# A scale-and-add kernel: HBM split in blocks of 72 and 56 rows, with a new order of loads and stores

## The chip, the cores and the metric

The kernel runs on one core of one Trainium2 chip. The metric is the device time of one execution in microseconds. Three runs of the kernel before gave 119.58, 119.69 and 119.91 us, a median of 119.69 us.

## What is computed

```python
B, S, D = 1024, 16, 512
x = normal(B, S, D) * 0.05          # bf16
y = normal(B, S, D) * 0.05          # bf16
gamma = 1e-4 * (normal(D) * 0.05)   # bf16

def reference(x, y, gamma):
    return x + gamma * y
```

With its first two dimensions flattened, each of `x`, `y` and the output is a matrix of 16,384 rows of 512 bf16 values, 1 KB a row and 16.78 MB a matrix. Two matrices are read and one is written: 50.33 MB.

## The kernel before

The 16,384 rows are shared out over the 128 partitions, 128 rows each. In this text "rows 4 to 68" means rows 4 to 68 of every partition, so a transfer of 64 rows moves 64 KB for each partition, 8.39 MB in all.

**Blocks.** `BLOCKS` (line 7) says which rows of HBM belong to a partition. The matrix is cut into three blocks of 4, 64 and 60 rows a partition. Within a block a partition's rows lie next to each other, so a transfer inside one block is one contiguous run for each partition. The function `rows_of` makes this view and asserts that a transfer stays within a block. As the work is elementwise, any such split gives the same output as long as `x`, `y` and the output use the same one.

**Transfers.** Two engines issue DMAs, each in the order of a list written out by hand. `SP` (lines 12 to 19) is the SyncE's: all of `y` and nearly all of `x`. `ACT` (line 20) is ScalarE's: the first four rows of `x`, `gamma`, and the three stores. An `x` entry has a fourth number, the row of the buffer `x_sb` at which it is placed. `x_sb` has 76 rows only, so the later loads of `x` overwrite rows that an addition has read. `y_sb` holds all 128 rows and is also where the result is made. `ring` (line 113) issues the lists and puts the waits in front: a load of `x` waits until the additions that free its place are done (`frees`), and a store waits until the additions of its own rows are done, both by counting the semaphore `s_add` in the order of the additions. `EARLY` moves the first two of SP's DMAs and the first of ScalarE's to the very start of the program, ahead of the start barrier.

**Hold and release.** `HOLD` names the load `y` 0 to 4. TensorE waits for its landing (line 147) and then raises one semaphore each for SP, ScalarE and VectorE (lines 148 and 149). SP's third DMA and ScalarE's second (`AHEAD`) wait for it. `RELEASE` names the load `x` 68 to 120. TensorE waits for its landing (line 157) and then raises `s_go`, for which the first store waits, and `s_rel`, for which VectorE waits.

**Compute.** `gamma` is copied to all partitions once: a matmul with a row of ones (line 152) and a copy out of PSUM (line 154). All other arithmetic is VectorE's. `PIECES` (line 9) cuts the 128 rows into pieces of 8, 16, 44, 52 and 8 rows, and the list `DVE` gives the order: `('m', c)` multiplies piece `c` of `y` by gamma in place (line 180), `('a', c)` adds `x` to it (line 189). The order is m0, m1, m2, a2, a0, a1, m3, m4, a3, a4.

Of the kernel before, what the change touches and what calls it, by code (L numbers as in the profile page):

```python
# [3 lines left out]

BLOCKS = [4, 64, 60]

PIECES = [8, 16, 44, 52, 8]


SP = [
    ('y', 0, 4),
    ('y', 4, 68),
    ('x', 4, 68, 4),
    ('y', 68, 128),
    ('x', 68, 120, 24),
    ('x', 120, 128, 0),
]
ACT = [('x', 0, 4, 0), ('g',), ('s', 4, 68), ('s', 0, 4), ('s', 68, 128)]  # L20

EARLY = (2, 1)

HOLD, AHEAD = ('y', 0, 4), (2, 1)

RELEASE = ('x', 68, 120, 24)

DVE = [('m', 0), ('m', 1), ('m', 2), ('a', 2), ('a', 0), ('a', 1), ('m', 3), ('m', 4), ('a', 3), ('a', 4)]
MULT, ADD = mybir.AluOpType.mult, mybir.AluOpType.add


def _take(sem, n, eng):


    return eng.wait_ge(sem, n).then_inc(sem, -n)  # L35


def kernel(
# [9 lines left out]
    nc = tc.nc  # L48
# [8 lines left out]
    rows = N // P  # L57
    n = len(PIECES)
    assert sum(PIECES) == rows
    starts = [sum(PIECES[:c]) for c in range(n + 1)]  # L60
    dt = xf.dtype
    edges = [sum(BLOCKS[:c]) for c in range(len(BLOCKS) + 1)]
    assert edges[-1] == rows

    def rows_of(t, a, b):

        c = max(c for c in range(len(BLOCKS)) if edges[c] <= a)
        assert b <= edges[c + 1]
# [6 lines left out]
    y_sb = nc.alloc_sbuf_tensor("y_sb", [P, rows, D], dt).ap()  # L75
    x_loads = [w for w in ACT + SP if w[0] == "x"]
    y_loads = [w for w in SP + ACT if w[0] == "y"]
    stores = [w for w in SP + ACT if w[0] == "s"]
    for loads in (x_loads, y_loads, stores):
# [7 lines left out]
    s_load = {w: sem("s_" + "_".join(map(str, w[:2]))) for w in x_loads + y_loads}  # L87
    s_held = {nc.sync: sem("s_held_sp"), nc.scalar: sem("s_held_act"), nc.vector: sem("s_held_dve")}
    s_add, s_go, s_rel, s_end, s_out = sem("s_add"), sem("s_go"), sem("s_rel"), sem("s_end"), sem("s_out")
    added = [a for kind, *a in DVE if kind == "a"]  # L90
    order = {a[0]: k for k, a in enumerate(added)}

    def meets(a, b, c, d):
        return a < d and c < b
# [4 lines left out]
    def x_at(row):  # L99
        return next(w[3] + row - w[1] for w in x_loads if w[1] <= row < w[2])  # L100
# [12 lines left out]
    def ring(eng, what, n_early, n_ahead):  # L113

        known, went = 0, False
        for k, w in enumerate(what):
            kind = w[0]
            if k == n_ahead:
                _take(s_held[eng], 1, eng)
            need = frees(w) if kind == "x" else pieces_of(w[1], w[2]) + list(w[3:]) if kind == "s" else []  # L120
            need = max((order[c] + 1 for c in need), default=0)
            if kind == "s" and not went:
                _take(s_go, 1, eng)
                went = True
            if need > known:
                eng.wait_ge(s_add, need)
                known = need
            if kind == "g":
                i = eng.dma_start(out=gamma_row, in_=gamma.unsqueeze(0)).then_inc(s_gamma, 16)
            elif kind == "x":  # L130
                to = x_sb[:, w[3] : w[3] + w[2] - w[1], :]
                i = eng.dma_start(out=to, in_=rows_of(xf, w[1], w[2])).then_inc(s_load[w], 16)
            elif kind == "y":
                r = slice(w[1], w[2])
                i = eng.dma_start(out=y_sb[:, r, :], in_=rows_of(yf, w[1], w[2])).then_inc(s_load[w], 16)
            else:
                r = slice(w[1], w[2])
                i = eng.dma_start(out=rows_of(of, w[1], w[2]), in_=y_sb[:, r, :]).then_inc(s_out, 16)
            if k < n_early:
                early.append(i.ins)  # L140

    ring(nc.sync, SP, EARLY[0], AHEAD[0])
    ring(nc.scalar, ACT, EARLY[1], AHEAD[1])


    nc.vector.memset(ones_row, 1.0).then_inc(s_ones, 1)  # L146
    _take(s_load[HOLD], 16, nc.tensor)
    for s_one in s_held.values():
        nc.tensor.sem_inc(s_one, 1)
    _take(s_ones, 1, nc.tensor)  # L150
    _take(s_gamma, 16, nc.tensor)
    nc.tensor.matmul(gamma_ps, ones_row, gamma_row, start=True, stop=True).then_inc(s_ps, 1)  # L152
# [3 lines left out]

    _take(s_load[RELEASE], 16, nc.tensor)
    nc.tensor.sem_inc(s_go, 1)
# [4 lines left out]
    def need(loads, c):  # L163
        for w in loads:
            if w not in landed and meets(starts[c], starts[c + 1], w[1], w[2]):
                if w == RELEASE:
                    _take(s_rel, 1, nc.vector)
                elif w == HOLD:
                    _take(s_held[nc.vector], 1, nc.vector)
                else:  # L170
                    _take(s_load[w], 16, nc.vector)
                landed.add(w)

    for kind, *args in DVE:
        c = args[0]
        yt = y_sb[:, starts[c] : starts[c + 1], :]
        if kind == "m":
            need(y_loads, c)
            g = gamma_sb[:, None, :].to_broadcast([P, PIECES[c], D])
            nc.vector.tensor_tensor(out=yt, in0=yt, in1=g, op=MULT).then_inc(s_dve, 1)  # L180
            open_mults += 1
        else:
# [4 lines left out]
            at = x_at(starts[c])  # L187
            xt = x_sb[:, at : at + PIECES[c], :]
            nc.vector.tensor_tensor(out=yt, in0=xt, in1=yt, op=ADD).then_inc(s_add, 1)  # L189
# [44 lines left out]
```

## Time and profile before

| what | us |
|---|---|
| median of three runs | 119.69 |
| span of the profiled execution, first to last instruction | 118.2 |
| VectorE busy in the span | 70.1 |
| of that, the five multiplies and the five additions | 34.7 each |
| TensorE busy | 0.6 |
| mean DMA rate over the span | 426 GB/s |

The profiled execution's own time is known by its span; what lies around the span, by comparison with the median of the runs, is about 1.5 us. "Busy" counts the arithmetic of an engine, not the issuing of DMAs or the waits. The page's DMA row gives, for 40 equal slices of the span, the mean busy share of the core's 16 DMA engines in tenths.

The timeline gives the issue times, which are needed to read the landings: SP issues `y` 0-4 and `y` 4-68 from 0.00 on, `x` 4-68 at 3.71 and `y` 68-128 at 4.09, and the last two loads of `x` from 55.37 on. ScalarE issues `x` 0-4 at 0.13, `gamma` at 3.90, and the three stores from 77.41 to 94.43. The page's list of DMA issues names each transfer with its size and the time from its issue to its landing; transfers of 64 rows are the ones without a size.

### The profile page before, as it was taken

How to read it: one execution, taken by the hardware profiler on the slowest of the kernel's cores; microseconds unless marked ns; L12 is line 12 of the kernel's file. 1: busy time of each engine (PE TensorE's matmuls, PEld its weight loads, DVE VectorE, ACT ScalarE, POOL GpSimd, SP SyncE). 2: the span in 40 equal slices, each digit the busy share in tenths (PEclk: the TensorE clock that was granted, in tenths of full speed). 3: DMA queues.
4: the chain of work that ended last, by engine and by line, in shares of the span. 5: the costliest groups of instructions: out<-in, count | busy, mean ns of one | idle time of the engine just before them, and what ended most of it. 6: DMA issues, size and time to landing. Idle time of an engine off the chain costs nothing. (4 is left out here: it accounts for less than half of the span.)

```text
span 118.2 us, 91 instructions
## 1 busy us (share of the span) xinstructions
PE 0.6 (0%) x1; PEld 0.1 (0%) x1; DVE 70.1 (59%) x12; POOL 0.2 (0%) x4
## 2 busy tenths in 40 slices
PE   0000100000000000000000000000000000000000
PEld 0000000000000000000000000000000000000000
DVE  0000200089999969999999999999999900000000
POOL 0000000000000000000000000000000000000000
DMA  6999889988899879879969696898899889799793
GB/s 248 461 666 399 355 355 399 665 355 355 355 599 466 355 333 624 374 333 499 499 288 576 288 576 288 360 637 355 355 576 488 355 355 510 333 582 416 333 499 166
DMA packets 1442, 50.33 MB, mean 426 GB/s; under 512 B 161, under 2 KB 162, under 8 KB 546
## 3 DMA queue, kind: packets, MB, share of 16 engines
q1 hardware_dynamic: 864, 33.03, 64.8%
q10 hardware_dynamic: 578, 17.30, 33.9%
HBM read 33.56 MB, written 16.78 MB: 426 GB/s over the span
## 5 line engine op out<-in xcount | busy, mean ns | idle before, releaser
L180 DVE TENSOR_TENSOR y_sb<-y_sb,gamma_sb 128x4096 bf16<-128x4096 bf16 (+3 forms) x5 | 34.7, 6981 | 10.9 <-DVEq L35 10.9
L189 DVE TENSOR_TENSOR y_sb<-x_sb,y_sb 128x4096 bf16<-128x4096 bf16 (+3 forms) x5 | 34.7, 6981 | 1.2 <-DVEq L35 1.1
L154 DVE CAST gamma_sb<-gamma_ps 128x512 bf16<-128x512 f32 x1 | 0.7, 692 | 10.2 <-DVEq L35 10.2
L146 DVE MEMSET ones_row<- 1x128 bf16 x1 | 0.2, 165 | 2.0 <-PEq L51 2.0
L152 PE MATMUL gamma_ps<-gamma_row,ones_row 1*128 1x512 bf16 x1 | 0.6, 581 | 11.6 <-PEq L35 11.6
L152 PEld LDWEIGHTS gamma_ps<-gamma_row,ones_row 1*128 1x128 bf16 x1 | 0.1, 101 | 11.6 <-issue 11.6
L218 POOL MEMSET const-bfloat16-1.0<- 128x1 bf16 x1 | 0.1, 101 | 0.0
L218 POOL MEMSET const-uint8-127<- 128x1 uint8 x1 | 0.1, 101 | 0.0
L218 POOL MEMSET const-float32-0.0<- 128x1 f32 x1 | 0.1, 98 | 0.2 <-issue 0.2
L218 POOL MEMSET const-float32-1.0<- 128x1 f32 x1 | 0.1, 98 | 0.0
## 6 DMA issues: line engine op xcount, KB each, us to landing
y_sb<-in_y_dram SPq DMA_DIRECT2D x1, 7680.0 KB, 57.3
out_dram<-y_sb ACTq DMA_DIRECT2D x1, 7680.0 KB, 23.8
x_sb<-in_x_dram SPq DMA_DIRECT2D x1, 6656.0 KB, 21.7
x_sb<-in_x_dram SPq DMA_DIRECT2D x1, 1024.0 KB, 22.0
y_sb<-in_y_dram SPq DMA_DIRECT2D x1, 512.0 KB, 3.4
x_sb<-in_x_dram ACTq DMA_DIRECT2D x1, 512.0 KB, 4.2
out_dram<-y_sb ACTq DMA_DIRECT2D x1, 512.0 KB, 22.3
y_sb<-in_y_dram SPq DMA_DIRECT2D x1, 23.4
```

The source lines that it names most:

```text
L146: nc.vector.memset(ones_row, 1.0).then_inc(s_ones, 1)
L152: nc.tensor.matmul(gamma_ps, ones_row, gamma_row, start=True, stop=True).then_inc(s_ps, 1)
L154: nc.vector.tensor_copy(out=gamma_sb, in_=gamma_ps).then_inc(s_dve, 1)
L180: nc.vector.tensor_tensor(out=yt, in0=yt, in1=g, op=MULT).then_inc(s_dve, 1)
L189: nc.vector.tensor_tensor(out=yt, in0=xt, in1=yt, op=ADD).then_inc(s_add, 1)
L218: nc = _bacc.Bacc("TRN2", target_bir_lowering=False, num_devices=1)
```

## The change

The blocks become 72 and 56 rows. SP's list begins with `y` 8 to 72 and `x` 8 to 72, which are also its two early DMAs. Then come `y` 72 to 128, `y` 0 to 8, `x` 72 to 128 and `x` 0 to 8. ScalarE's list begins with `gamma`, which is now its early DMA, and has the three stores behind it: 8 to 72, 0 to 8, 72 to 128. There is no `HOLD` any more, so its wait on TensorE, the three raised semaphores and the three waits for them are gone. `RELEASE` names `x` 72 to 128. The pieces are 8, 12, 52 and 56 rows, in the order m1, m2, a2, a1, m3, m0, a3, a0.

```diff
-BLOCKS = [4, 64, 60]
-
-PIECES = [8, 16, 44, 52, 8]
-
+BLOCKS = [72, 56]
+
+PIECES = [8, 12, 52, 56]
 
 SP = [
-    ('y', 0, 4),
-    ('y', 4, 68),
-    ('x', 4, 68, 4),
-    ('y', 68, 128),
-    ('x', 68, 120, 24),
-    ('x', 120, 128, 0),
+    ('y', 8, 72),
+    ('x', 8, 72, 8),
+    ('y', 72, 128),
+    ('y', 0, 8),
+    ('x', 72, 128, 20),
+    ('x', 0, 8, 0),
 ]
-ACT = [('x', 0, 4, 0), ('g',), ('s', 4, 68), ('s', 0, 4), ('s', 68, 128)]
+
+ACT = [('g',), ('s', 8, 72), ('s', 0, 8), ('s', 72, 128)]
 
 EARLY = (2, 1)
 
-HOLD, AHEAD = ('y', 0, 4), (2, 1)
-
-RELEASE = ('x', 68, 120, 24)
-
-DVE = [('m', 0), ('m', 1), ('m', 2), ('a', 2), ('a', 0), ('a', 1), ('m', 3), ('m', 4), ('a', 3), ('a', 4)]
+HOLD = None
+
+AHEAD = (None, None)
+
+RELEASE = ('x', 72, 128, 20)
+
+DVE = [('m', 1), ('m', 2), ('a', 2), ('a', 1), ('m', 3), ('m', 0), ('a', 3), ('a', 0)]
...
-    _take(s_load[HOLD], 16, nc.tensor)
-    for s_one in s_held.values():
-        nc.tensor.sem_inc(s_one, 1)
+    if HOLD:
+        _take(s_load[HOLD], 16, nc.tensor)
+        for s_one in s_held.values():
+            nc.tensor.sem_inc(s_one, 1)
```

From the new lists follow the waits: `x` 72 to 128 waits for the first addition (a2), `x` 0 to 8 for none of its own; the store of 8 to 72 waits for `s_go` and the first two additions, the store of 0 to 8 for all four.

## The prediction

> **What bounds the kernel now.** I read the page from the top down to its DMA rows, then the table of landings, then narrow windows at the opening and at the seams between transfers, and last the VectorE (DVE) groups by form.
>
> ```profile
> span 118.2 us, 91 instructions
> PE 0.6 (0%) x1; PEld 0.1 (0%) x1; DVE 70.1 (59%) x12; POOL 0.2 (0%) x4
> ...
> DMA packets 1442, 50.33 MB, mean 426 GB/s; under 512 B 161, under 2 KB 162, under 8 KB 546
> ```
>
> DVE works 59% of the span; the DMA engines move 50.33 MB in it. In the windows a packet is counted whole where it starts, so only long windows, or windows of short packets, give a rate.
>
> ```profile
> 0.90:1.00 0.10, 0.00 (x0) 0.00 (x0) 0.00 (x0) 0.00 (x0) 1.00 0.00 0
> 1.00:2.00 1.00, 0.00 (x0) 0.00 (x0) 0.01 (x1) 0.00 (x0) 1.00 0.94 352
> 2.00:2.90 0.90, 0.00 (x0) 0.00 (x0) 0.16 (x1) 0.00 (x0) 1.00 1.00 401
> 2.90:3.60 0.70, 0.00 (x0) 0.00 (x0) 0.00 (x0) 0.00 (x0) 1.00 1.00 410
> 3.60:4.00 0.40, 0.00 (x0) 0.00 (x0) 0.00 (x0) 0.00 (x0) 1.00 6.53 2744
> 1.00:3.60 2.60, 0.00 (x0) 0.00 (x0) 0.17 (x1) 0.00 (x0) 1.00 0.98 384
> 23.50:42.80 19.30, 0.00 (x0) 0.00 (x0) 18.43 (x3) 0.00 (x0) 1.00 1.00 431
> 76.90:78.40 1.50, 0.00 (x0) 0.00 (x0) 1.35 (x2) 0.00 (x0) 1.00 0.98 415
> 1.00:118.20 117.20, 0.58 (x1) 0.10 (x1) 70.08 (x12) 0.00 (x0) 1.00 1.00 429
> ```
>
> The last two columns are DMA share and GB/s. Nothing moves before 1.00; from then on the share is 1.00. So the end is set by the bytes, by the rate of each kind of row, and by the 1.00 us ahead of the first packet. Rows of 64 KB go at 431 GB/s; the two 4-row loads at the opening go at 384 (352, 401, then 410). Rows of 8 KB (`x` 120 to 128) go at 415; the same window moved by 0.1 us gives 426.
>
> ```profile
> y_sb<-in_y_dram SPq DMA_DIRECT2D x1, 7680.0 KB, 57.3
> x_sb<-in_x_dram SPq DMA_DIRECT2D x1, 6656.0 KB, 21.7
> x_sb<-in_x_dram SPq DMA_DIRECT2D x1, 1024.0 KB, 22.0
> x_sb<-in_x_dram ACTq DMA_DIRECT2D x1, 512.0 KB, 4.2
> out_dram<-y_sb ACTq DMA_DIRECT2D x1, 512.0 KB, 22.3
> y_sb<-in_y_dram SPq DMA_DIRECT2D x1, 23.4
> x_sb<-in_x_dram SPq DMA_DIRECT2D x1, 39.5
> out_dram<-y_sb ACTq DMA_DIRECT2D x1, 21.5
> ```
>
> With the issue times of the timeline these are landings: x 0-4 at 4.3, y 4-68 at 23.8 (DVE's first multiply starts at 23.95), x 4-68 at 43.2 (issue 3.71), y 68-128 at 61.4 (4.09), x 68-120 at 77.1 (55.37), x 120-128 at 79.6 (57.6), s 4-68 at 98.9 (77.41), s 0-4 at 100.1 (77.8), and the end at 118.2. Each follows the one before by its bytes over about 431 GB/s. The chain of waits names only 11% "issue" and 3% DVE, as transfers are no part of it; it is no guide here.
>
> **The change, part by part.** Bytes stay 50.33 MB, so each term is a difference from 431 GB/s.
>
> *Opening.* The two 4-row loads (1.05 MB) leave. At 384 GB/s they take 2.73 us, at 431 they would take 2.43: 0.30 us. Of that, 0.13 is the row size (1.05 MB at the settled 410 takes 2.56) and goes. The other 0.17 is the first two microseconds being slow, which may be the fate of whatever load comes first. Ends: -0.30 and -0.13; the trace has no opening with 64 KB rows, so I take the middle, -0.21.
>
> *Start of the first packet.* The first issue is again SP's first instruction; y 0-4 had its first packet 1.00 us after issue. For a 64 KB row as opener the nearest other row is s 4-68, issued at 77.41:
>
> ```profile
> 78.70:79.20 0.50, 0.00 (x0) 0.00 (x0) 0.50 (x1) 0.00 (x0) 1.00 5.09 2196
> 79.20:79.40 0.20, 0.00 (x0) 0.00 (x0) 0.20 (x1) 0.00 (x0) 1.00 0.00 0
> ```
>
> All its first rows start between 78.7 and 79.2, at most 1.8 us after issue, part of it queueing behind x 120-128. Ends: 0 and +0.8; I take 0, as y 0-4 is an opener and the store is not.
>
> *Unevenness.* The 64 KB rows of the 16 DMA engines begin anywhere in 3.60 to 4.00 (the 2744 window; the next 0.1 us has none), a spread of up to 0.4 made in part by the small rows and the seam between two queues; the slowest engine sets the end. Ends 0 and -0.15; taken -0.05.
>
> *8-row pieces.* There are three (y, x, store) where there was one. Each is 1.05 MB at 415 to 426: 2.53 to 2.46 us against 2.43. Two more cost +0.06 to +0.20; taken +0.10. The 4-row store goes: at 410 it would lose 0.06 us to 431, by its landing (1.2 us) nothing; taken -0.04.
>
> *Big pieces.* 64 rows stay 64; 60, 52 and 60 become 56, 56 and 56. The windows and landings give 428 to 434 GB/s for rows of 52 to 64 KB: 0. The 72 KB stride between partitions is not in the trace; 4, 60 and 64 KB strides are, the last two without a difference. Ends -0.1 and +0.6 (1% of the 58 us of 64-row transfers); taken 0, from those rows.
>
> Sum: -0.21 - 0.05 + 0.10 - 0.04 = **-0.20 us**. The profiled span is 118.2; the median of the runs, 119.69, lies 1.5 above it, which is start and end outside the span and is not touched. 118.2 becomes 118.0, **119.5 by the runs**.
>
> **What is costed at nothing, and its cover.**
>
> ```profile
> L189 DVE TENSOR_TENSOR y_sb<-x_sb,y_sb 128x26624 bf16<-128x26624 bf16 x1 | 14.0, 14024 | 0.1
> L189 DVE TENSOR_TENSOR y_sb<-x_sb,y_sb 128x22528 bf16<-128x22528 bf16 x1 | 11.9, 11892 | 1.1 <-DVEq L35 1.1
> L189 DVE TENSOR_TENSOR y_sb<-x_sb,y_sb 128x4096 bf16<-128x4096 bf16 x2 | 4.6, 2286 | 0.0
> ```
>
> These rows give 0.52 ns an element: 12 rows 3.35 us, 52 rows 14.02, 56 rows 15.09, 8 rows 2.29. The new timetable: y 8-72 lands at 21.1 (23.8 less 2.7), x 8-72 at 40.5, y 72-128 at 57.4, y 0-8 at 59.9, x 72-128 at 76.8, x 0-8 at 79.3, s 8-72 at 98.7, s 0-8 at 101.2, end 118.0.
>
> Hold removed (PE's wait and three increments, one take each on SP, ACT, DVE): SP issues y 72-128 and y 0-8 at about 2 us, behind 38 us of queued loads. Gamma goes out at 0.1; it took from its issue at 3.90 to the matmul at 11.56, 7.7 us, among 64 KB rows. Twice that is still ahead of 21.1, where the first multiply needs it.
>
> x 72-128 waits on SP for the first add, with x 0-8 queued behind. Multiplies end at 21.2 + 3.35 + 14.02 = 38.6, the add runs from 40.8 to 54.8, and the queue runs dry near 59.9: 5.1 us ahead, where before it was 6.0 (55.37 to 61.4). An opener needs 1.0; margin about 4. Beyond it, each microsecond shows in full.
>
> The stores wait for x 72-128 as for x 68-120 before: issue 0.34 after landing (77.41 against 77.07) behind an 8-row load of the same 2.5 us. The margin is unchanged.
>
> New wait: s 0-8 needs the last add, and s 72-128 stands behind it on ACT. DVE is free at 75.5, the adds start at 77.4 and end at 77.4 + 15.09 + 2.29 = 94.8; s 8-72 lands at 98.7. 3.9 us less at most 1.8 from issue to first row (the store above) leaves 2.1 or more; each microsecond beyond that shows in full. Before it was 94.43 against 100.1.
>
> **Where the skill differs.** The Trainium skill ("DMA: Bandwidth & Descriptors", Anatomy of one DMA) charges each transfer about 2.0 us beside bytes/436; one of 11 transfers fewer would be an estimated -2.0, 117.7. Here x 120-128 lands 2.5 us after its predecessor with 1.05 MB, not 4.4, so behind a full queue that charge is hidden. The same page (Queues, rings and completion order) speaks against the change: each DMA engine alternates between queues packet by packet, so a store released early would trade 64 KB rows for x 0-8's 8 KB rows, and that load would land up to some 19 us late, an estimate. In this trace x 120-128, in the same place, landed on time.
>
> **Rivals.** *The whole opening loss goes, and the spread too*: -0.30 - 0.15 + 0.06 - 0.06 = -0.45, **119.25**. For it: the rate climbs to 410 within 2 us though rows stay 4 KB, and 64 KB rows lose less to any fixed gap. Against: the first microsecond is slow whatever the size.
>
> *The first 64 KB rows come late* (slower): the place is 0 to 1.00, where nothing else moves, so it costs one for one. From a first packet at 1.56 us (0.2 gain and 0.36 used up) it is slower; at 1.8, the store's bound, it is -0.2 + 0.8 = +0.6, **120.3**. For it: no small load opens the queue. Against: y 0-4 needed 1.00 with the same 128 rows to describe, and SP's first two issues took 0.85 together.
>
> *x 0-8 caught behind the store*, which is issued 2.2 us before x 0-8 lands: if the queues take turns, each 8 KB row that is overtaken waits 2.43 us (16 rows of 64 KB at 431). The last add can start at 92.5 and x 0-8 lands at 79.3, so it decides from six of the eight rows of an engine on; with all, the add starts near 98.7, s 0-8 moves at 98.7 + 2.3 + 1.0 = 102: +3.3, **122.8**. For it: gamma's 1 KB took 7.7 us among 64 KB rows. Against: x 120-128 landed 2.5 us after its predecessor with a store issued as early.
>
> **How the numbers follow.** Forecast (-0.05 to -0.35 us) 0.42; whole gain 0.36; late first row (or a slow 72 KB stride, +0.6, same size) 0.18; caught load 0.04. A measurement of this kernel tells about 0.3% (0.36 us) from no change. The forecast is inside it, the first rival is faster, the other two slower: faster 0.36, same 0.42, slower 0.22. Its own range is 119.3 to 119.7; with the gain at its bound, 0.45, and the runs' spread (119.58 to 119.91) the low end is 119.1; half-way into the late first row gives 119.95. Beyond the two ends I leave 2 in 10.
>
> **What would show it.** Right: no packet before 1.00 and some by 1.1; first DVE multiply near 21.2; x 72-128 issued near 54.8; the last add ending near 94.8; share 1.00 throughout; span 118.0. Wrong: a first packet after 1.3, a window of low share near 60, 79 or 98.5, a rate under 428 in the stretch from 21 to 40, or a span above 118.5 or below 117.7.

## The result: 120.26 us, 0.5% slower, and the profile after

The changed kernel takes 120.26 us (median of five runs, 120.15 to 120.33) against 119.69 before: a ratio of 1.0046, with a 95% interval of 1.0035 to 1.0056. The forecast was 119.5, its range ended at 119.95; the time lies 0.3 us above that end. The profiled execution has a span of 118.9 us (118.2 before).

The head of the page of the changed kernel:

```profile
span 118.9 us, 81 instructions
...
DMA packets 1298, 50.33 MB, mean 423 GB/s; under 512 B 145, under 2 KB 146, under 8 KB 146
```

There are fewer instructions and fewer packets for the same 50.33 MB, and a lower mean rate: 423 GB/s, not 426. Where the rate is lost is told by the list of DMA issues of the changed kernel (last column: us from issue to landing; the line without a size is `y` 8-72):

```profile
y_sb<-in_y_dram SPq DMA_DIRECT2D x1, 7168.0 KB, 56.4
x_sb<-in_x_dram SPq DMA_DIRECT2D x1, 7168.0 KB, 22.1
out_dram<-y_sb ACTq DMA_DIRECT2D x1, 7168.0 KB, 22.8
y_sb<-in_y_dram SPq DMA_DIRECT2D x1, 1024.0 KB, 58.5
x_sb<-in_x_dram SPq DMA_DIRECT2D x1, 1024.0 KB, 24.2
out_dram<-y_sb ACTq DMA_DIRECT2D x1, 1024.0 KB, 6.3
y_sb<-in_y_dram SPq DMA_DIRECT2D x1, 22.0
```

With the issue times of the timeline the landings stand against the forecast timetable so:

| transfer | forecast | measured | behind |
|---|---|---|---|
| y 8-72 | 21.1 | 22.0 | 0.9 |
| y 72-128 | 57.4 | 58.3 | 0.9 |
| y 0-8 | 59.9 | 60.8 | 0.9 |
| x 72-128 | 76.8 | 77.8 | 1.0 |
| x 0-8 | 79.3 | 80.2 | 0.9 |
| end | 118.0 | 118.9 | 0.9 |

The whole miss is there when the first load lands, and nothing is added after it. So the opening has to be looked at. Windows of the changed kernel there (the last two columns are DMA share and GB/s; a packet counts whole in the window in which it starts):

```profile
0.90:1.30 0.40, 0.00 (x0) 0.00 (x0) 0.00 (x0) 0.00 (x0) 1.00 5.30 1802
1.30:2.70 1.40, 0.00 (x0) 0.00 (x0) 0.17 (x1) 0.00 (x0) 1.00 0.62 234
...
3.90:4.30 0.40, 0.00 (x0) 0.00 (x0) 0.00 (x0) 0.00 (x0) 1.00 3.03 1311
4.30:4.80 0.50, 0.00 (x0) 0.00 (x0) 0.00 (x0) 0.00 (x0) 1.00 2.43 1051
```

1802 GB/s over 0.40 us are 11 rows of 64 KB, 234 over 1.40 are 5: each of the 16 DMA engines starts its first row here, 11 of them by 1.30 as forecast, the other 5 later. The share times the width of the window is the time that an engine spends, on average, on the rows started in it: 5.30 x 0.40 + 0.62 x 1.40 = 2.99 us for one first row, against 2.43 for a 64 KB row at 431 GB/s. The second rows, 8 in each of the last two windows, take the normal 2.43 (3.03 x 0.40 + 2.43 x 0.50), but start over a stretch of up to 0.9 us; before, the 64 KB rows began within 0.4 us.

### The profile page after: what moved, and what is told of

Same layout as the page of the kernel before. It is cut to its first block, busy times and chain, and to the rows that moved or that the text cites. A ratio compares the mean times of both kernels' runs of the same rounds, so it can differ in the third digit from the quotient of the medians.

```text
span 118.9 us, 81 instructions
## 1 busy us (share of the span) xinstructions
PE 0.6 (0%) x1; PEld 0.1 (0%) x1; DVE 69.9 (59%) x10; POOL 0.2 (0%) x4
## 2 busy tenths in 40 slices
DMA packets 1298, 50.33 MB, mean 423 GB/s; under 512 B 145, under 2 KB 146, under 8 KB 146
## 5 line engine op out<-in xcount | busy, mean ns | idle before, releaser
L183 DVE TENSOR_TENSOR y_sb<-y_sb,gamma_sb 128x6144 bf16<-128x6144 bf16 (+3 forms) x4 | 34.6, 8686 | 13.2 <-DVEq L37 13.2
L192 DVE TENSOR_TENSOR y_sb<-x_sb,y_sb 128x26624 bf16<-128x26624 bf16 (+3 forms) x4 | 34.6, 8689 | 4.4 <-DVEq L37 4.4
```

## The experiments

Ratios are to the kernel before, run on the same chip.

**A small piece first, another stride, a later second load, and the hold by itself.** Four runs ask which part of the new opening is slow.

`y` 0-8 in front of `y` 8-72:

```diff
 SP = [
+    ('y', 0, 8),
     ('y', 8, 72),
     ('x', 8, 72, 8),
     ('y', 72, 128),
-    ('y', 0, 8),
     ('x', 72, 128, 20),
```

> The changed kernel with y 0-8 put in front of y 8-72; nothing else moves. Three theories of the 0.9 us that the changed kernel's first load lands later than forecast (22.0 against 21.1 us). Row size (the engines begin slowly, and with 64 KB rows every engine has its first long row under way then): the opener's 8 KB rows take the loss instead, the span falls from 118.9 to about 118.2, the time from 120.26 to about 119.6. Stride (72 KB between partitions): the 8 KB rows have the same stride, so span 118.9, time 120.2. Crowding (the next load is issued 0.4 us after the first, nothing held back): the next load still is, span 118.9, time 120.2.

Measured: 122.14 us, ratio 1.0213 (1.0197 to 1.0230), span 120.4. No theory expected this, and the opening is not the reason: the first multiply starts at 24.45, and less the 2.43 us that `y` 0-8 takes at 431 GB/s this is 22.0, while the changed kernel's starts at 22.15. From the list of DMA issues of this run:

```profile
y_sb<-in_y_dram SPq DMA_DIRECT2D x1, 7168.0 KB, 58.3
x_sb<-in_x_dram SPq DMA_DIRECT2D x1, 7168.0 KB, 21.2
```

`y` 72-128, issued at 2.28, lands at 60.6 and is now the last transfer ahead of `x` 72-128, which waits for the first addition and is issued at 57.96, 2.6 us earlier. `x` 72-128 lands at 79.2, 18.6 us after its predecessor; in the changed kernel it was 17.0 (77.8 after 60.8). Two windows of this run show the rows of 56 KB on either side of the seam, first the 16 first rows of `x` 72-128, then the 16 last ones of `y` 72-128:

```profile
59.70:61.20 1.50, 0.00 (x0) 0.00 (x0) 1.50 (x2) 0.00 (x0) 1.00 1.76 612
57.40:58.10 0.70, 0.00 (x0) 0.00 (x0) 0.70 (x2) 0.00 (x0) 1.00 3.05 1311
```

The engines come to `x` 72-128 within 1.5 us, where they had come to the last rows of `y` within 0.7, and its first rows take 1.76 x 1.50 = 2.64 us on average where the ones before took 3.05 x 0.70 = 2.14: they start late, and they are long, as at the opening. With a lead of 2.6 us the load came 1.6 us late, so it would have wanted about 4.2, an estimate from these rows. The changed kernel has 5.1: the late place of `y` 0-8 is cover (work queued ahead of a load while it gets going) that it needs.

The opening is read separately. This run, then the kernel before:

```profile
1.00:2.40 1.40, 0.00 (x0) 0.00 (x0) 0.17 (x1) 0.00 (x0) 1.00 0.94 223
```

```profile
1.00:2.40 1.40, 0.00 (x0) 0.00 (x0) 0.17 (x1) 0.00 (x0) 1.00 0.94 354
```

The 8 KB rows of the opener begin at 223 GB/s; the 4 KB rows of the kernel before had 354 in the same window, at the same share. A small row is not enough.

Blocks of 8, 64 and 56 rows, so that `y` 8-72 has a stride of 64 KB:

```diff
-BLOCKS = [72, 56]
+BLOCKS = [8, 64, 56]
```

> The changed kernel with blocks of 8, 64 and 56 rows, so that y 8-72 is whole rows of a 64 KB stride; the list of transfers is the same. Row size: first rows of the opener take 3.0 us as in the changed kernel, span 118.9, time 120.2. Stride: span 118.2, time 119.6. Crowding: span 118.9, time 120.2.

Measured: 120.08 us, 1.0030 (1.0019 to 1.0041), span 118.6. By the same windows as above its first rows take 5.93 x 0.40 + 0.51 x 1.40 = 3.09 us. The first row is as slow, so the 72 KB stride is not what makes it long. The time is 0.2 us better than the changed kernel's; the intervals overlap, so whether the stride costs up to 0.2 us in another way is not shown.

`x` 8-72 issued after the start barrier:

```diff
-EARLY = (2, 1)
+EARLY = (1, 1)
```

> The changed kernel with only y 8-72 and gamma ahead of the start barrier, so x 8-72 is issued at 1.9 us instead of 0.4. Row size: no change, span 118.9, time 120.2. Stride: no change, 118.9 and 120.2. Crowding: the first rows take 2.5 us instead of 3.0, span 118.3, time 119.7.

Measured: 120.31 us, 1.0047 (1.0035 to 1.0058), span 119.2; first rows 6.04 x 0.40 + 0.52 x 1.40 = 3.14 us, though the second load goes out at 1.73 instead of 0.42. The issue at 0.42 is not the cause. Holding the second load back until the first rows are done, near 4.3, was not tried.

The kernel before without its hold:

```diff
-HOLD, AHEAD = ('y', 0, 4), (2, 1)
+HOLD, AHEAD = None, (None, None)
```

> The kernel before without its hold: x 4-68, y 68-128 and gamma are issued right after the start barrier, at about 2 us instead of 3.7 to 4.1. Row size: span as before, 118.2, time 119.7. Stride: the same, 118.2 and 119.7. Crowding: the 4-row loads of the opening are slowed, span 118.6 or more, time 120.1 or more.

Measured: 119.74 us, 0.9999 (0.9990 to 1.0007), span 118.4. The hold is worth nothing either way.

**Is it where the opener's rows lie in HBM?** Of these openers only those of 4 KB rows in one contiguous stretch were quick. Twins with the same transfers and an opener of 4 KB rows, once in its own block, once in the block of 72 rows:

```diff
-BLOCKS = [72, 56]
+BLOCKS = [4, 4, 64, 56]      # the first twin only
 SP = [
+    ('y', 0, 4),
     ('y', 8, 72),
     ('x', 8, 72, 8),
     ('y', 72, 128),
-    ('y', 0, 8),
+    ('y', 4, 8),
     ('x', 72, 128, 20),
-    ('x', 0, 8, 0),
+    ('x', 0, 4, 0),
+    ('x', 4, 8, 4),
 ]
-ACT = [('g',), ('s', 8, 72), ('s', 0, 8), ('s', 72, 128)]
+ACT = [('g',), ('s', 8, 72), ('s', 0, 4), ('s', 4, 8), ('s', 72, 128)]
```

> The changed kernel with y 0-4 as the opener (4 KB rows) and y 4-8 left in the late place of y 0-8, in blocks of 4, 4, 64 and 56 rows, so that the opener is one contiguous stretch of 0.5 MB. Its twin has the same transfers in blocks of 72 and 56 rows. First long row late (the opening debt goes with the row size): both open alike, their first packets near 0.2 to 0.5 us each and the rate near 384 GB/s over the first 2.4 us; span 118.2 for both. Spread (an opener whose rows lie 64 or 72 KB apart in HBM opens about 0.4 us worse than one in a contiguous stretch, whatever its row size): this one opens as the kernel before did, span 118.2, time 119.6.

> The same transfers in the changed kernel's blocks of 72 and 56 rows: the opener's 4 KB rows lie 72 KB apart. Row size: as the twin, span 118.2, time 119.6. Spread: the first packets take about 0.6 us longer than a 4 KB row needs, the span is about 0.4 us above the twin's, 118.6, time 120.1. If x 72-128 runs out of cover (it has 4 rows of y less in front of it than in the changed kernel), both twins lose the same and only their difference counts.

Measured: contiguous 120.17 us, 1.0042 (1.0029 to 1.0055); spread 120.90 us, 1.0099 (1.0076 to 1.0121). The opening of the contiguous twin, then that of the spread one:

```profile
1.00:2.40 1.40, 0.00 (x0) 0.00 (x0) 0.17 (x1) 0.00 (x0) 1.00 0.90 287
```

```profile
1.00:2.40 1.40, 0.00 (x0) 0.00 (x0) 0.17 (x1) 0.00 (x0) 1.00 0.91 176
```

The same rows on busy engines, and 287 against 176 GB/s. The direction is that of the spread theory, but the totals are not: the contiguous twin was expected at 119.6. The totals can't be read cleanly. With only 4 rows in the place of 8, `x` 72-128 is issued about 4 us before the queue runs dry (issue at 56.48, landing 20.9 later, less 17.0 for its own bytes, leaves 3.9), near the limit that the first run gave, and the runs scatter (120.01 to 120.47, and 120.44 to 121.59 for the spread twin). The openings can be compared: the first multiply starts at 22.94 and 23.38, and less 1.22 us for `y` 0-4 this is 21.7 for the contiguous twin, near the kernel before (23.95 less 2.43: 21.5), and 22.2 for the spread one, as in the changed kernel (22.15). Much of what the contiguous twin gains at the opening it loses behind it; whether to the cover or to its smaller pieces is not shown. So the next run changes the spread in a kernel whose cover isn't touched.

The kernel before in blocks of 68 and 60 rows; its opener now lies 68 KB apart:

```diff
-BLOCKS = [4, 64, 60]
+BLOCKS = [68, 60]
```

> The kernel before with blocks of 68 and 60 rows in place of 4, 64 and 60: the list of transfers is the same to the row, only the 4-row opener (y 0-4, x 0-4) now lies 68 KB apart from partition to partition in HBM instead of in one stretch of 0.5 MB. Spread: the opening takes 0.25 to 0.4 us longer, span 118.5, time 120.0. If the spread is not the cause: as before, 118.2 and 119.7. Aliasing (the slow openings had strides that are multiples of 8 KB, which 68 KB is not): as before, 118.2 and 119.7.

Measured: 119.96 us, 1.0018 (1.0009 to 1.0026), span 118.6, and the same kernel once more on another chip, with this expectation:

> The kernel before with blocks of 68 and 60 rows once more, on the chip of the run beside it. All theories: 119.95 us, about 0.2 above the kernel before.

119.93 us, 1.0018 (1.0009 to 1.0027). Windows of the first of the two:

```profile
1.00:2.40 1.40, 0.00 (x0) 0.00 (x0) 0.17 (x1) 0.00 (x0) 1.00 0.92 205
1.00:3.60 2.60, 0.00 (x0) 0.00 (x0) 0.17 (x1) 0.00 (x0) 1.00 0.96 301
```

301 GB/s, where the kernel before had 384, are (384 - 301) x 2.6 / 431 = 0.50 us of work not done by 3.6. By the runs the spread costs 0.0018 x 119.75 = 0.2 us; part of the difference is that the profiled execution before had a good opening (without the hold the same opener gave 304 GB/s in the shorter window, not 354). The edit also moves the 64-row transfers from a stride of 64 KB to one of 68, but from the first multiply to the end nothing is lost (24.38 to 118.6, against 23.95 to 118.2). Spread is a cause, and about 0.2 us of the 0.55.

**Is it the multiple of 8 KB in the stride?**

```diff
-BLOCKS = [72, 56]
-PIECES = [8, 12, 52, 56]
+BLOCKS = [73, 55]
+PIECES = [9, 12, 52, 55]
...
-    ('y', 8, 72),
+    ('y', 9, 73),
```

with all other bounds moved by one row in the same way.

> The changed kernel with blocks of 73 and 55 rows, its short pieces of 9 rows: a stride of 73 KB. Aliasing: the first 64 KB rows take 2.5 us as in the middle of the kernel, span 118.5, time 119.9. Spread: first rows of 3.0 us as in the changed kernel, span 118.9, time 120.2.

Measured: 120.23 us, 1.0037 (1.0025 to 1.0049), first rows 6.16 x 0.40 + 0.51 x 1.40 = 3.18 us. Beside it the changed kernel as it stands:

> The changed kernel as it stands, beside the others on their chip. All theories: time 120.2, span 118.9, first rows of about 3.0 us; what it adds is a second profile of the opening, by which the others on this chip are read.

120.29 us, 1.0042 (1.0030 to 1.0054), span 119.0. So the multiple of 8 KB is not the reason.

**A tighter opener**, 2 KB rows in 0.25 MB, without the hold:

```diff
-BLOCKS = [4, 64, 60]
-PIECES = [8, 16, 44, 52, 8]
+BLOCKS = [2, 64, 62]
+PIECES = [8, 14, 44, 54, 8]
...
-    ('y', 0, 4),
-    ('y', 4, 68),
+    ('y', 0, 2),
+    ('y', 2, 66),
...
```

with the other bounds at 4 and 68 moved to 2 and 66 in the same way.

> The kernel before without its hold and with blocks of 2, 64 and 62 rows: an opener of 2 KB rows in one stretch of 0.25 MB. Spread: the tighter opener is no worse and may be up to 0.15 us better, time 119.55 to 119.75. Row size (2 KB rows move more slowly than 4 KB rows): 0.1 to 0.2 us worse, 119.8 to 119.9.

Measured: 119.79 us, 1.0003 (0.9994 to 1.0011). Neither better nor worse; no version found here beats the kernel before.

**The remaining 0.3 us.** The changed kernel is at 1.0042 to 1.0046, the kernel with a spread but small opener at 1.0018. What is left is either the long first row or the late 8-row pieces. This run has the long first row and no further 8-row piece:

```diff
 BLOCKS = [68, 60]
-PIECES = [8, 16, 44, 52, 8]
+PIECES = [4, 20, 44, 52, 8]
 SP = [
-    ('y', 0, 4),
     ('y', 4, 68),
     ('x', 4, 68, 4),
     ('y', 68, 128),
+    ('y', 0, 4),
     ('x', 68, 120, 24),
-    ('x', 120, 128, 0),
+    ('x', 0, 4, 0),
+    ('x', 120, 128, 4),
 ]
-ACT = [('x', 0, 4, 0), ('g',), ('s', 4, 68), ('s', 0, 4), ('s', 68, 128)]
+ACT = [('g',), ('s', 4, 68), ('s', 0, 4), ('s', 68, 128)]
```

The additions of rows 0 to 4 move behind the big ones, and there is no hold.

> The layout of the run with blocks of 68 and 60 rows, but with y 4-68 as the first load, no hold, and the 4-row loads of y and x moved to late places, so no 8-row piece is added beyond x 120-128. It stands beside that run repeated. Long opener (64 KB rows leave the DMA engines out of step from the start, beyond what the spread costs): spread of the engines' ends 0.4 us or more above their mean, time 120.2 to 120.3, as the changed kernel. Late 8-row pieces (they make the rest of the changed kernel's loss): time as the run with blocks of 68 and 60 rows, 119.9 to 120.0.

Measured: 120.58 us, 1.0071 (1.0057 to 1.0084), span 119.3. Windows of this run at its opening, and then where the 16 DMA engines start the last row (60 KB) of the last store:

```profile
0.90:1.30 0.40, 0.00 (x0) 0.00 (x0) 0.00 (x0) 0.00 (x0) 1.00 5.61 1802
1.30:2.70 1.40, 0.00 (x0) 0.00 (x0) 0.17 (x1) 0.00 (x0) 1.00 0.62 234
```

```profile
115.20:115.70 0.50, 0.00 (x0) 0.00 (x0) 0.00 (x0) 0.00 (x0) 1.00 0.28 123
115.70:116.00 0.30, 0.00 (x0) 0.00 (x0) 0.00 (x0) 0.00 (x0) 1.00 4.72 2048
116.00:116.30 0.30, 0.00 (x0) 0.00 (x0) 0.00 (x0) 0.00 (x0) 1.00 1.42 614
116.30:116.80 0.50, 0.00 (x0) 0.00 (x0) 0.00 (x0) 0.00 (x0) 1.00 0.57 246
```

The same windows of the first run with the small opener in blocks of 68 and 60 rows, whose last store has the same rows:

```profile
115.20:115.70 0.50, 0.00 (x0) 0.00 (x0) 0.00 (x0) 0.00 (x0) 1.00 2.55 1106
115.70:116.00 0.30, 0.00 (x0) 0.00 (x0) 0.00 (x0) 0.00 (x0) 1.00 3.31 1434
116.00:116.30 0.30, 0.00 (x0) 0.00 (x0) 0.00 (x0) 0.00 (x0) 1.00 0.00 0
116.30:116.80 0.50, 0.00 (x0) 0.00 (x0) 0.00 (x0) 0.00 (x0) 1.00 0.00 0
```

The first rows take 5.61 x 0.40 + 0.62 x 1.40 = 3.11 us. At the end, GB/s times width over 61,440 bytes gives the engines that start their last row in each window: 1, 10, 3 and 2 with the long opener, 9, 7, 0 and 0 with the small one. As a group they are later, and two are far behind; the end waits for them. The loss is there at the first landing: `y` 4-68 lands at 22.4, and from there to the end this run takes 96.9 us, as the changed kernel does from 22.0 on. The stride is the same as in the run with the small opener, so the opener's size is a second cause, and the loss does not need late 8-row pieces. Its size here, 0.0053 x 119.75 = 0.6 us, is twice what is missing in the changed kernel; the two lists differ in more than the opener. Most of the other 0.3 us is in the opening too (22.4, against 22.0 and 22.2 in the two profiles of the changed kernel); why it is larger here stayed open.

## Why the prediction was wrong, step by step

**The opening** is the term that failed. The prediction put it at -0.21 us between ends of -0.30 and -0.13: the small rows' loss would go, and the slow first two microseconds would at worst stay. It took 0.17 us of the old opening's loss for the price of being first, whatever is loaded, and 0.13 for the price of a small row. Together they were the price of a good opener. With rows spread over HBM the same small transfers cost about 0.2 us more (1.0018, twice). The changed kernel loses about 0.3 beyond that (1.0042 to 1.0046 less 1.0018), and its landings leave only the opening for it; that a long opener costs time at equal stride is shown, by 0.6 us in another list, so the division is less certain than the sum.

One figure compares all openings: the start of the first multiply, less the time of the small loads ahead of it at 431 GB/s. It is 21.5 to 21.7 in the four profiles whose opener has rows of 2 or 4 KB in one stretch, 21.9 to 22.2 in the four with small rows spread out, and 21.9 to 22.5 in the six with 64 KB rows. By the runs the opening and the unevenness below together are about +0.5 instead of -0.26 (+0.57 in all, less the 0.06 of the small pieces), and no end of the opening term allowed a loss, though no row of the trace showed an opening with wide rows. The start of the first packet was given an end of +0.8; the opening was owed an end above zero as well.

**The first packet** was put at 1.00 us, and is there (11 rows in 0.90 to 1.30). The rival "the first 64 KB rows come late" had the right place and the right sign, and 0.18 of the chance, but the wrong event: its condition, a first packet after 1.56, was not met. The queue starts on time; its first rows are long, 2.99 us instead of 2.43, and five engines begin after 1.30.

**The unevenness** was put at -0.05, because the seam between two queues would go. It became worse: the second rows start over up to 0.9 us, where 64 KB rows had started within 0.4, and the run with a long opener shows two engines still behind at the end. How much of the loss this is can be read from the trace, which has 16 landing times for each transfer, as many as there are DMA engines. For `y` 8-72 their mean is 21.60 in both profiles of the changed kernel, and the last comes 0.42 and 0.60 us after the mean. For `y` 4-68 of the kernel before, less 2.43 us, the mean is 21.16 (21.31 without the hold), and the last comes 0.22 us after it (0.23). So at the first landing the mean engine has lost 0.3 to 0.4 us, and the slowest another 0.2 to 0.4. The lag stays: at the end the last landing is 0.38 and 0.52 us after the mean in the changed kernel, 0.64 in the run with the long opener at 68 KB, and 0.24 and 0.31 in the two runs with the small one.

**The 8-row pieces** at +0.05 each: `y` 0-8 lands 2.5 us after its predecessor (60.8 after 58.3), `x` 0-8 2.4 (80.2 after 77.8), as forecast within what tenths can tell.

**The big pieces and the 72 KB stride** at 0: right. From 22.0 to the end the changed kernel takes 96.9 us, and the forecast timetable took 96.9 (21.1 to 118.0). At the opening, strides of 64 and 73 KB changed no first row.

**The covers** all held, with the opening's 0.9 us added: the first multiply at 22.15 (forecast 21.2), `x` 72-128 issued at 55.66 (54.8), the last addition done at 95.7 (94.8). One margin was taken too large: the prediction gave `x` 72-128 about 4 us to spare, counting 1.0 us from issue to first packet. The run with `y` 0-8 in front shows that about 4.2 us are wanted there, so the margin was nearer to 1.

**Hold and gamma** at nothing: right (0.9999 without the hold; gamma's matmul at 7.52, long before 22.15). The rival of an opening loss that goes in full had the sign wrong. The load caught behind the store did not occur: `x` 0-8 landed 2.4 us after its predecessor beside a store issued at 78.09. The prediction had held against the change that the Trainium skill ("DMA: Bandwidth & Descriptors", Queues, rings and completion order) lets each DMA engine take turns between queues, packet by packet; no such turn delayed this load. The 2.0 us for each transfer that the prediction takes from the same page (Anatomy of one DMA) are fitted there on DMAs issued from GpSimd; behind the full queue here `y` 0-8 took no such time either.

## What to carry to other kernels

In a kernel whose transfers never pause, the first load deserves a look of its own: small rows that lie together in HBM opened better here than spread ones, by 0.2 us, and than long ones, by 0.4 to 0.85 us, which nothing later gave back. When a trace shows only one kind of opening, its rate is no price for another kind, and the bound has to allow a loss. An opening can also leave the DMA engines out of step, and the slowest one sets the end. Before a short transfer is moved to the front, see which later load was using it as cover.

## What the runs showed of the hardware that was not expected

- The rate of the first 1.4 us depends on how the opener's rows lie: 287, 304 and 354 GB/s for 4 KB rows in one stretch, 176 to 223 for 4 and 8 KB rows 68 or 72 KB apart. The first packet starts at 1.0 us in all of them. Why spread rows start slowly was not found. For the long first rows of the changed kernel, a stride that is a multiple of 8 KB, or not a power of two, and the issue of the next load at 0.42 are ruled out as the reason.
- The Trainium skill ("DMA: Bandwidth & Descriptors", Latency and other measured facts) lists low rates, in copies between HBM tensors, for row pitches of 512 KiB and more at large powers of two. No run here has such a pitch; at 64, 72 and 73 KB the long first rows took 3.09, 2.99 and 3.18 us, no better off the power of two.
- The first 64 KB row of a DMA engine takes 2.99 to 3.18 us on average when it opens the kernel and 2.43 afterwards.
- What the DMA engines are out of step by after the first load, they keep: the last of 16 landings came 0.42 us after their mean at 22.0 and 0.38 at the end, and 0.67 and 0.64 in the run with the long opener at 68 KB.
- A load issued 2.6 us before the queue's last landing came 1.6 us late, and its first 56 KB rows took 2.64 us on average instead of 2.14. With 5.1 us none was lost. About 4 us are wanted, an estimate from these two.
